# A Fourier filter and a gated MLP on one core: the opening's pieces in another order, the identity matrix made by POOL instead of loaded

## The chip, the cores and the metric

The kernel runs on one core of a Trainium2 chip. The metric is the device time of one execution in microseconds; the median of three runs is compared. A profiled execution has its own device time and, inside it, a span from its first to its last instruction. Engines: PE multiplies matrices (PEld loads its weights), DVE works elementwise, ACT evaluates functions, POOL does small copies and sums over partitions, SP issues the DMAs. Each engine works through its own queue in order; they wait for one another through semaphores.

## The reference

```python
xn = layernorm(x)                                # x is [1, 2048, 448], f32
A  = irfft2(rfft2(xn) * (w_r + 1j * w_i))        # over the 2048 rows and 448 columns
g  = xn @ W_gate;  u = xn @ W_up                 # [448, 1792] each
B  = (where(g > 0, g, 0) * u) @ W_down           # [1792, 448]
return x + A + B
```

## The kernel before

Every f32 operand of a matmul is split into a high and a low f16 part, and each product is three f16 passes. The 2048 rows lie as 16 row tiles of 128 partitions, numbered n2; tiles n2, n2+4, n2+8, n2+12 form a chunk q, and the chunks are worked in the order 0, 2, 1, 3. A row tile is normalised, split (`hi`, `lo`), and transposed into `Tq[q]`, [128, 9, 512]. The 1792 hidden columns are 14 tiles f in groups of 5, 5 and 4; a *unit* is one f with one chunk q: 20 matmuls of 128x512 and its share of four half passes into the PSUM tile `gu` (g=0 gate, g=1 up). A weight tile `wst` (256 KB) is squared and summed by ACT (`w_sq`), summed over partitions by POOL (`w_sum`, a PartitionAllReduce), turned into a power of two by DVE (`w_scale`), and split by ACT (`w_hi`) and DVE (`w_lo`) into the f16 tile `wt`. The second matmul with `W_down` (`dn`) and the Fourier part (`fx`) follow chunk by chunk, woven into the units by a planner that spends estimated costs (`add(cost, ...)`, `run_bg`).

The first five units cannot be planned that way, because rows and weights arrive while they are used. So a string, `OPENING`, names small pieces one after the other, and inside `tc.manual_schedule` each engine gets its instructions in exactly that order. `lx4` loads row tile 4, `lw` the next weight tile, `st4` its statistics, `sqA`/`rsA` the reciprocal deviation of tiles 0 and 4 (`B`: 8 and 12), `xn4` the normalised f32 row, `hi4`/`lo4` the split, `cp4` two POOL copies inside the split tile, `tpA4`/`tpB4` transposes on PE against an identity matrix `id_t`, `vevA4`/`aevA4` the evictions to `Tq` by DVE or ACT, `wsqW0g1`, `parW0g1`, `wscW0g1`, `whiW0g1`, `wloW0g1` the five weight steps, `hh10`, `lh10`, `hl10` parts of unit 0 (first digit g, second the half of the 512 columns), `gu1g0` half g=0 of unit 1, `kwN` and `warm` matmuls on a zero tile that nothing reads.

Of the kernel before, what the change touches and what calls it, by code (L numbers as in the profile page):

```python
# [8 lines left out]

# [16 lines left out]
NWARM = 19  # L26
# [4 lines left out]
lx0 lx4 lw lid lw lx8 lx12 lw lw lw lw lx2 lx10 lx6 lx14 lwd0 lwd1 lwd2 lwd3 lwd4 warm st0 st4 sqA rsA hi4  # L31
xn4 xn0 wsqW0g0 cp4 st8 hi0 parW0g0 st12 wsqW0g1 cp0 tpA0 lo0 tpA4 kw1 wscW0g0 sqB tpB0 kw6 parW0g1 wsqW1g0
rsB whiW0g0 vevB0 lo4 wsqW1g1 xn12 tpB4 kw3 hi8 parW1 wscW0g1 xn8 whiW0g1 cp8 vevA0 vevA4 hi12 tpA8 vevB4
hh10 hh00 lo8 wsqW2g1 cp12 tpA12 hl00 lo12 aevA12 tpB8 aevA8 hl10 wloW0g0 lw aevB8 tpB12 wscW1 lh00 aevB12
wloW0g1 lw lfd hh01 hh11 whiW1g0 st2 lh01 lh10 whiW1g1 hl01 wloW1g0 lw hl11 wsqW2g0 wloW1g1 lw ly0 ly4 ly8
ly12 d90 d94 d98 d912 lh11 wsqW3g0 st10 parW2 hp0 st14 wsqW3g1 gu1g0 st6 wdq0 parW3 wscW2 sqC wscW3 whiW2g0 rsC gu1g1 re0
wloW2g0 whiW3g1 tm0 whiW2g1 xn6 wsqW4g0 xn2 gu2g0 wloW2g1 hi2 re1 xn10 gh0 wloW3g1 whiW3g0 tm1 gu2g1 wdq1
wloW3g0 hi10 xn14 lo2 hi14 hi6 cp14 hp2 wsqW4g1 cp2 lo6 gu3g0 cp10 dm2 lo14 re2 parW4 wdq2 cp6 wscW4 tm2
whiW4g0 dm14 lo10 wdq4 gu3g1 wloW4g0 gh1 dm10 gl0 whiW4g1 gl1 dm6 gu4g0 re3 wloW4g1 wdq3 tm3 wdp gh3
wdsc gh2 gu4g1 gl2 wdh1 wdh2 wdl1 wdh0 wdl2 hp4 gl3 re4 wdh3 tm4 wdl0 gh4 wdh4 gl4 wdl3 wdl4  # L40
# [43 lines left out]
def _constants():  # L84
# [55 lines left out]
    ident = np.eye(128, dtype=np.float16)  # L140
    return dict(ident=ident, c_fd=c_fd, c_fm=np.ascontiguousarray(c_fm), c_im=c_im, c_row=c_row,
# [4 lines left out]
def tile_gfnet_reglu(ctx: ExitStack, tc: tile.TileContext, x, xr, wgu, wd, wf, ident, c_fd, c_fm, c_im, c_row, c_id,  # L146
# [100 lines left out]
    def ln_stats(q, j):  # L247
        n2 = q + 4 * j
        st = ft([128, 6], F32, "bst", 2)
        V.bn_stats(st, xr_t[n2])  # L250
        if j == 0:
            mv[q] = ft([128, 4, 2], F32, "mv", 2)
        V.bn_aggr(mv[q][:, j, :], st)

    rst = {}

    def ln_sd(q, js=(0, 1, 2, 3)):
        w = ft([128, 5, 4], F32, "rs", 3)
        n = len(js)
        rst[q, js[0]] = w[:, :, 0:n], mv[q][:, js[0]:js[-1] + 1, :]  # L260
        A.activation(w[:, 0, 0:n], rst[q, js[0]][1][:, :, 1], AF.Sqrt, bias=eps)

    def ln_rstd(q, js=(0, 1, 2, 3), bias=False):
        w, m = rst[q, js[0]]
        sd, r0, t, r, nm = (w[:, i] for i in range(5))
        V.reciprocal(r0, sd)
        V.scalar_tensor_tensor(t, m[:, :, 1], 1e-5, r0, op0=OP.add, op1=OP.mult)
        V.scalar_tensor_tensor(t, t, -0.5 * 2048, r0, op0=OP.mult, op1=OP.mult)
        V.scalar_tensor_tensor(r, t, 1.5 * 2048, r0, op0=OP.add, op1=OP.mult)
        if bias:  # L270
            V.scalar_tensor_tensor(nm, m[:, :, 0], -1.0, r, op0=OP.mult, op1=OP.mult)
        elif q in CHUNKS[2:]:
            V.tensor_scalar(nm, m[:, :, 0], -1.0, None, op0=OP.mult)
        for i, j in enumerate(js):
            rst[q, j] = r[:, i:i + 1], nm[:, i:i + 1], m[:, i, 0:1]
# [9 lines left out]

    def ln_xn(n2):
        xn_b[n2] = free.pop(0)
        xn[n2] = xn_b[n2].rearrange("p g c k -> p (g c k)")[:, 0:D]
        r, _, mean = rst[n2 % 4, n2 // 4]
        V.tensor_scalar(xn[n2], xr_t[n2], mean, r, op0=OP.subtract, op1=OP.mult)  # L290

    def ln_hi(n2, fused=False):
        new_tt(n2)
        o = tt[n2].rearrange("p a b -> p (a b)")[:, 0:D]
        r, nm, _ = rst[n2 % 4, n2 // 4]
        if fused:
            A.activation(o, xr_t[n2], AF.Identity, scale=r, bias=nm)
        else:
            A.activation(o, xn[n2], AF.Copy)
# [6 lines left out]
    def ln_norm(n2):  # L306
        xn_b[n2] = free.pop(0)
        xn[n2] = xn_b[n2].rearrange("p g c k -> p (g c k)")[:, 0:D]
        r, nm, _ = rst[n2 % 4, n2 // 4]
        A.activation(xn[n2], xr_t[n2], AF.Identity, bias=nm)  # L310
        new_tt(n2)
        A.activation(tt[n2].rearrange("p a b -> p (a b)")[:, 0:D], xn[n2], AF.Copy, scale=r)
        ln_copy(n2)
        free.append(xr_b.pop(n2))

    def ln_lo(n2):
        x, t = xn[n2], tt[n2].rearrange("p a b -> p (a b)")
        x2, t2 = [v[:, None, :].to_broadcast([128, 2, 64]) for v in (x[:, 384:448], t[:, 384:448])]
        if n2 % 4 in CHUNKS[2:]:
            r = rst[n2 % 4, n2 // 4][0]  # L320
            V.scalar_tensor_tensor(t[:, 512:896], x[:, 0:384], r, t[:, 0:384], op0=OP.mult, op1=OP.subtract)
            V.scalar_tensor_tensor(tt[n2][:, 3:9:5, 64:128], x2, r, t2, op0=OP.mult, op1=OP.subtract)
        else:
            V.tensor_tensor(t[:, 512:896], x[:, 0:384], t[:, 0:384], op=OP.subtract)
            V.tensor_tensor(tt[n2][:, 3:9:5, 64:128], x2, t2, op=OP.subtract)
        G.tensor_copy(tt[n2][:, 8, 0:48].rearrange("p (a b) -> p a b", b=16), tt[n2][:, 4:7, 112:128])
        free.append(xn_b.pop(n2))

# [351 lines left out]
    def w_scale(f, gs=(0, 1)):  # L680
        sc = mt([128, 2], F32, "wsc", 6)
        e = eg[:, f, gs[0]:gs[-1] + 1]
        half_exponent(e, state["wm", f][:, 1, gs[0]:gs[-1] + 1])
        shift_exponent(sc[:, 0:len(gs)], e, -1, 188)
        for i, k in enumerate(gs):
            wsc[f, k] = sc[:, i:i + 1]

# [8 lines left out]
    def wd_sq(i, f):  # L696
        if i == 0:
            state["wdm"] = mt([128, 2, NR], F32, "wdm", 1)
        squares(wdst[f], state["wdm"][:, 0, i:i + 1])
# [43 lines left out]
    def gu_half(f, q, g, start, prev):  # L743


        rows, b = TOP[g]
        m = P.matmul(hps[f, q][:, g, 0:512], wt[f, g][rows, 7, :], Tq[q][rows, b, :], start=start, stop=not start).ins  # L747
# [17 lines left out]
    def gu_halves(f, q, mate):  # L765
        gu_open(*mate)
        m = last["P"]
        for i in range(4):
            with tc.high_priority(offset=2000 if i else 0):
                m = gu_half(*((f, q) if i > 1 else mate), 1 - i % 2, i < 2, m)  # L770
        opened.add(mate)
# [81 lines left out]
    def ln_chunk(q):  # L853
        for j in range(4):
            add(0.63, ln_stats, q, j)
        add(0.0, ln_sd, q)
        add(0.6, ln_rstd, q)
# [194 lines left out]
    def keep_warm(n):  # L1052
        for _ in range(n):
            P.matmul(wps, warm[:, 0:128], warm, start=True, stop=True)

    pieces = {"lid": lambda: nc.sync.dma_start(id_t, ident), "lfd": lambda: nc.sync.dma_start(fd_t, c_fd),
              "lw": load_wn, "warm": lambda: keep_warm(NWARM),
              **{f"kw{n}": (lambda n=n: keep_warm(n)) for n in (1, 3, 6)},
# [3 lines left out]
    def piece(name, fn, *a):  # L1062
        pieces[name] = lambda: fn(*a)

    for c, q in enumerate(CHUNKS[:2]):
        for js, tag in (((0, 1), "A"), ((2, 3), "B")) if c == 0 else (((0, 1, 2, 3), "C"),):
            piece("sq" + tag, ln_sd, q, js)
            piece("rs" + tag, ln_rstd, q, js, c == 0)
        for j in range(4):
            n2 = q + 4 * j  # L1070
            for tag, fn, *a in (("lx", load_xr), ("ly", load_x), ("st", ln_stats, j), ("xn", ln_xn),
                                ("hi", ln_hi, c == 0), ("cp", ln_copy), ("lo", ln_lo), ("dm", ln_dma), ("d9", ln_dma9),
                                ("tpA", ln_tp, (0, 1, 2)), ("tpB", ln_tp, (4, 5, 6, 3, 7))):
                piece(f"{tag}{n2}", fn, *((q,) if tag == "st" else (n2,)), *a)
# [5 lines left out]
    def gu_slab(f, g):  # L1080
        if f % 2 == 0 and g == 0:
            gu_open(f, q)
        gu_full(f, q, (g,), slice(0, 512), f % 2 == 0, f % 2 == 1)

    for f in groups[0]:
# [5 lines left out]
        piece(f"wscW{f}", w_scale, f)  # L1091
# [4 lines left out]
        for g in range(2):  # L1096
# [4 lines left out]
            if f == 0:  # L1101
                piece(f"parW{f}g{g}", w_sum, f, (g,))
                piece(f"wscW{f}g{g}", w_scale, f, (g,))
# [4 lines left out]
    with tc.manual_schedule(engines={mybir.EngineType.PE, mybir.EngineType.DVE, mybir.EngineType.Activation,  # L1108
# [4 lines left out]
        gu_open(0, q)  # L1113
        for name in OPENING.split():
            pieces[name]()
# [64 lines left out]
_ORDER = ["x", "xr", "wgu", "wd", "wf", "ident", "c_fd", "c_fm", "c_im", "c_row", "c_id"]  # L1180
# [42 lines left out]
```

## Time and profile before

| what | value |
|---|---|
| median of 3 runs | 447.95 us (447.57 to 448.4) |
| profiled execution, device time | 448.09 us |
| its span | 446.3 us |
| PE busy in the span | 437.7 us (98%) |
| DVE, ACT, POOL busy | 381.9, 188.2, 34.3 us |
| first matmul into `gu` | 14.44 us after the span's start |

The 1.8 us between device time and span lie around the first and last instruction. "Idle before, releaser" names the instruction whose end let a waiting engine go on. Durations of single instructions overlap a little with the next one on the same engine.

### The profile page before, as it was taken

The page shows a single profiled execution, that of the slowest core. Times are in us where ns is not written, and L with a number is a line of the kernel's source. Part 1 is how long each engine was busy: PE and PEld are TensorE (multiplying, and loading weights), DVE is VectorE, ACT ScalarE, POOL GpSimd, SP SyncE. Part 2 cuts the span into 40 slices and gives each one's busy share as a digit, 9 for nine tenths or more (in the row PEclk, how much of TensorE's full clock was granted, in tenths as well). Part 3 has the DMA queues.
Part 4 walks back from the last instruction along what each step waited for, and adds up shares of the span by engine and source line. Part 5 has one row for each costly group of instructions (what it writes and reads, how often), then busy time and mean ns, then how long its engine had stood idle before and what let it go on. Part 6 is the DMA issues. An engine that isn't in the chain of part 4 may idle for free.

```text
span 446.3 us, 7350 instructions
## 1 busy us (share of the span) xinstructions
PE 437.7 (98%) x2625; PEld 219.1 (49%) x2625; DVE 381.9 (86%) x958; ACT 188.2 (42%) x398; POOL 34.3 (8%) x89
## 2 busy tenths in 40 slices
PE   6999999999999999999999999999999999999996
PEld 2544555545455444444444444444445555555654
DVE  5989698999858899999999999987998799875443
ACT  5887263732643774323132255263334133244130
POOL 2320030210000310000000310100000000000000
PEclk9999999999999999999999999999999999999999
DMA  7939985040001462431302100011121121101212
GB/s 248 312 88 269 368 266 116 16 92 2 1 2 48 140 198 81 133 117 45 98 29 85 41 0 2 0 43 63 41 71 35 58 79 35 53 13 50 82 47 82
DMA packets 39228, 39.61 MB, mean 89 GB/s; under 512 B 18470, under 2 KB 35096, under 8 KB 39192
## 3 DMA queue, kind: packets, MB, share of 16 engines
q1 hardware_dynamic: 39192, 39.15, 28.6%
q8 instruction: 20, 0.33, 0.3%
q14 instruction: 16, 0.13, 0.1%
HBM read 24.38 MB, written 3.67 MB: 63 GB/s over the span
## 4 chain that ended last, share of the span: by engine, by line
PE 91%; DMA 3%; DVE 3%; issue 1%; SPq 0%; ACT 0%; POOL 0%; DVEq 0%; ACTq 0%
PE gu L740 51%; PE dn L808 26%; PE gu L747 3%; PE fx L639 2%; PE fx L368 2%; PE fx L658 2%; DMA wst<-in_wgu 2%; PE fx L398 2%; DMA y<-in_xr 1%; PE dn L836 1%; DVE wt L694 1%; PE gu L836 1%; DVE g L781 0%; DVE y L290 0%; DVE xy L814 0%
## 5 line engine op out<-in xcount | busy, mean ns | idle before, releaser
L740 PE MATMUL gu<-T,wt 128*128 128x512 f16 (+1 forms) x1140 | 255.6, 375 | 0.2 <-DVE wt L694 0.2
L740 PEld LDWEIGHTS <-wt 128*128 128x128 f16 x1140 | 108.7, 98 | 130.7 <-issue 9.8
L808 PE MATMUL dn<-wdt,h 128*128 128x448 f16 x624 | 127.0, 352 | 0.0
L808 PEld LDWEIGHTS <-h 128*128 128x128 f16 x624 | 60.3, 98 | 56.4 <-issue 0.4
L777 ACT ACTIVATE g<-gu 128x512 f32<-128x512 f32 x56 | 33.2, 593 | 92.4 <-PE gu L747 54.3
L785 ACT ACTIVATE h<-g 128x512 f16<-128x512 f32 x56 | 34.9, 626 | 58.2 <-DVE g L781 58.1
L781 DVE SCALAR_TENSOR_TENSOR g<-gu,g 128x512 f32<-128x512 f32 x56 | 38.3, 684 | 15.3 <-ACT g L777 15.2
L789 DVE TENSOR_TENSOR h<-g,h 128x512 f16<-128x512 f32 x56 | 38.3, 685 | 8.2 <-ACT h L785 8.0
L814 DVE SCALAR_TENSOR_TENSOR xy<-dn,dsc,xy 128x448 f32<-128x448 f32 x46 | 31.0, 676 | 12.3 <-PE dn L808 7.8
L189 POOL PARTITION_ALL_REDUCE wm<-wm x15 | 11.7, 779 | 167.8 <-ACT junk L186 167.8
L623 ACT ACTIVATE vt<-y,fsc 128x456 f16<-128x456 f32 x16 | 10.8, 673 | 27.9 <-PE fx L639 23.7
L690 ACT ACTIVATE wt<-wst,wsc 128x512 f16<-128x512 f32 x28 | 19.3, 714 | 5.6 <-DVE wsc L196 5.6
L694 DVE SCALAR_TENSOR_TENSOR wt<-wst,wsc,wt 128x512 f16<-128x512 f32 x28 | 20.4, 744 | 0.0
L186 ACT ACTIVATE junk<-wst 128x512 bf16<-128x512 f32 x28 | 17.4, 621 | 0.2
L747 PE MATMUL gu<-T,wt 64*128 64x512 f16 x112 | 17.0, 381 | 0.1
L663 DVE SCALAR_TENSOR_TENSOR xy<-fx,fsc,xy 128x448 f32<-128x448 f32 x16 | 10.8, 680 | 7.2 <-PE fx L658 7.2
L389 ACT ACTIVATE Xh<-X 128x456 f16<-128x456 f32 x16 | 9.3, 579 | 17.7 <-DVE X L387 8.7
L404 DVE TENSOR_TENSOR y<-y,y 128x456 f32<-128x456 f32 x22 | 13.8, 627 | 0.2
L639 PEld LDWEIGHTS <-vt 128*128 128x128 f16 x192 | 12.0, 98 | 4.0 <-issue 0.8
L250 DVE BATCH_NORM_STATS2 bst<-y 128x6 f32<-128x448 f32 x16 | 9.7, 612 | 4.9 <-DMA y<-in_xr 4.9
L405 DVE TENSOR_TENSOR y<-y,y 128x456 f32<-128x456 f32 x22 | 13.8, 626 | 0.1
L639 PE MATMUL fx<-im,vt 128*128 128x128 f16 x192 | 13.5, 219 | 0.0
(131 smaller groups left out, 476.9 us busy)
## 6 DMA issues: line engine op xcount, KB each, us to landing
sw<-y SPq DMA_DIRECT2D x64, 112.2 KB
wst<-in_wgu SPq DMA_DIRECT2D x28, 256.0 KB
wf<-in_wf SPq DMA_DIRECT2D x16, 228.0 KB
y<-in_xr SPq DMA_DIRECT2D x16, 224.0 KB
xy<-in_x SPq DMA_DIRECT2D x16, 224.0 KB
out<-xy SPq DMA_DIRECT2D x15, 224.0 KB
wdst<-in_wd SPq DMA_DIRECT2D x14, 224.0 KB
fm<-in_c_fm SPq DMA_DIRECT2D x4, 256.0 KB
```

The source lines that it names most:

```text
L186: A.activation(mt([128, 512], BF16, "junk")[:, 0:src.shape[-1]], src, AF.Square, scale=SQ, accum_out=acc)
L639: P.matmul(o, v[:, h, w], m[:, c, :], start=(i == 0), stop=(i == 2), skip_group_check=True)
L690: A.activation(w[:, 0:4, :], wst[f, g], AF.Copy, scale=wsc[f, g])
L694: V.scalar_tensor_tensor(w[:, 4:8, :], st, sc, w[:, 0:4, :], op0=OP.mult, op1=OP.subtract)
L740: last["P"] = P.matmul(hps[f, q][:, g, cs], wt[f, g][:, a, :], Tq[q][:, b, cs], start=(start and i == 0), stop=(stop and i == len(seq) - 1 ...
L747: m = P.matmul(hps[f, q][:, g, 0:512], wt[f, g][rows, 7, :], Tq[q][rows, b, :], start=start, stop=not start).ins
L777: last["A"] = A.activation(g1s[f, q], hps[f, q][:, 0, :], AF.Relu, scale=2.0 ** -22).ins
L781: last["V"] = V.scalar_tensor_tensor(g1, hps[f, q][:, 1, :], 2.0 ** -22, g1, op0=OP.mult, op1=OP.mult).ins
L785: A.activation(ht[f, q][:, 0, :], g1s[f, q], AF.Copy)
L789: V.tensor_tensor(h[:, 1, :], g1s.pop((f, q)), h[:, 0, :], op=OP.subtract)
L808: last["P"] = P.matmul(ps[:, 0:D], ht[f, q][:, a, js], wdt[f][:, b, :], start=(i == 0), stop=(i == n - 1)).ins
L814: last["V"] = V.scalar_tensor_tensor(xy[:, n2, cs], dps[n2][:, cs], dsc[:, g:g + 1], xy[:, n2, cs], op0=OP.mult, op1=OP.add).ins
```

## The change

The string is replaced. In words:

- The four row tiles of chunk 0 are loaded ahead of the first weight tiles; the other rows, the `xy` tiles, `fd_t` and the `W_down` tiles come later among the weights.
- `id_t` is no longer loaded (`lid`): the piece `mkid` has POOL clear it and write the diagonal with an affine select.
- Statistics, deviation and weight scale become pieces of one instruction each (`bn`/`ag`, `ra` to `rd`, `wex`/`wsc`), `lo` becomes `lo`/`lp`; the negated mean is its own piece `ng`.
- Row tiles 0 and 4 are centred by ACT (`xc`) and scaled by the split; tiles 8 and 12 and chunk 2 are normalised by DVE (`xn`) and copied by ACT.
- Unit 1 is issued in six pieces (`uh`, `um`, `ul` for each g) instead of two, some of them ahead of unit 0's half passes.
- 24 matmuls on the zero tile at the start and 4 later, instead of 19 and 10.
- Later chunks take their statistics two tiles at a time.

```diff
-NWARM = 19
+NWARM = 24
-lx0 lx4 lw lid lw lx8 lx12 lw lw lw lw lx2 lx10 lx6 lx14 lwd0 lwd1 lwd2 lwd3 lwd4 warm st0 st4 sqA rsA hi4
-xn4 xn0 wsqW0g0 cp4 st8 hi0 parW0g0 st12 wsqW0g1 cp0 tpA0 lo0 tpA4 kw1 wscW0g0 sqB tpB0 kw6 parW0g1 wsqW1g0
...
+lx0 lx4 bn0 bn4 ag0 ag4 warm ngA lx8 lx12 sqA xc0 xc4 raA rbA rcA rdA bn8 hi0 cp0 lw lw mkid lw bn12 hi4 ag8 cp4 lw
+tpA0 ag12 lo0 tpA4 sqB lp0 raB wsqW0g1 parW0g1 lx2 tpB0 lo4 lp4 lw wsqW0g0 rbB vevB0 wexW0g1 rcB parW0g0 wsqW1g0
+tpB4 kw4 vevA0 rdB wscW0g1 lw wexW0g0 whiW0g1 lw vevA4 wscW0g0 xn12 hh10 whiW0g0 vevB4 hl10 lx14 xn8 hh00 lw hl00
...
+    def ln_xc(n2):
+        xn_b[n2] = free.pop(0)
+        xn[n2] = xn_b[n2].rearrange("p g c k -> p (g c k)")[:, 0:D]
+        A.activation(xn[n2], xr_t[n2], AF.Identity, bias=rst[n2 % 4, n2 // 4, "m"])
...
+        A.activation(tt[n2].rearrange("p a b -> p (a b)")[:, 0:D], xn[n2], AF.Copy, scale=rst[n2 % 4, n2 // 4])
...
-    pieces = {"lid": lambda: nc.sync.dma_start(id_t, ident), "lfd": lambda: nc.sync.dma_start(fd_t, c_fd),
+    pieces = {"mkid": lambda: make_identity(nc, id_t), "lfd": lambda: nc.sync.dma_start(fd_t, c_fd),
...
+    def gu_part(g, n):
+        if (1, q) not in hps:
+            gu_open(1, q)
+        gu_full(1, q, (g,), slice(0, 512), n == 0, n == 2, (seq1[0:3], seq2, seq1[3:6])[n])
```

The function that `mkid` calls, on a [128, 128] f16 tile (sq is 128):

```python
def make_identity(nc, identity):
    nc.gpsimd.memset(identity, 0.0)
    nc.gpsimd.affine_select(out=identity, in_=identity, compare_op=mybir.AluOpType.not_equal, fill=1.0,
                            base=0, pattern=[[-1, sq]], channel_multiplier=1)
```

What the edit becomes on POOL is seen only in the program that is built from it. POOL before, from the first row copy to the second partition sum (`tt` are the split row tiles, `wm` the sums of squares; the plain `ISA` row is an instruction that names the code library that POOL needs next, here the one with index 1):

```order
L303 COPY tt0_100<-tt0_100 128x48 [waits Activation_49]
L304 COPY tt0_100<-tt0_100 128x64
L189 ISA
L189 ISA wm_182<-wm_182 128x1 [waits Activation_49]
L303 COPY tt1_101<-tt1_101 128x48 [waits Activation_49]
L304 COPY tt1_101<-tt1_101 128x64
L326 COPY tt1_101<-tt1_101 128x48 [waits DVE_49]
L189 ISA wm_182<-wm_182 128x1 [waits Activation_49]
```

It stands once, ahead of the first of 15 partition sums. POOL after, the same place (the library named ahead of the select has index 0, the one ahead of the sum index 1):

```order
L329 COPY tt0_100<-tt0_100 128x48 [waits Activation_49]
L330 COPY tt0_100<-tt0_100 128x64
masks.py:197 MEMSET id_t_97 128x128
masks.py:199 ISA
masks.py:199 AFFINE_SELECT id_t_97<-id_t_97 128x128 [waits Pool_49]
L329 COPY tt1_101<-tt1_101 128x48 [waits Activation_49]
L330 COPY tt1_101<-tt1_101 128x64
L354 COPY tt0_100<-tt0_100 128x48 [waits DVE_49]
L190 ISA
L190 ISA wm_199<-wm_199 128x1 [waits Activation_49]
L354 COPY tt1_101<-tt1_101 128x48 [waits DVE_49]
L190 ISA wm_199<-wm_199 128x1 [waits Activation_49]
```

The identity and a second library row now stand between the first row copy and the first partition sum. DVE before, around the first weight scale (`eg`, `wsc` from the sums `wm`; `rs` the deviations, `mv` the statistics; `T0` is the transposed chunk, `fx` the transposes' PSUM):

```order
L325 TENSOR_TENSOR tt1_101<-y9_75,tt1_101 128x2x64
L192 TENSOR_SCALAR eg_89<-wm_182 128x1 [waits Pool_49]
L196 TENSOR_SCALAR wsc_211<-eg_89 128x1 [waits DVE_49]
L266 RECIPROCAL rs_214<-rs_214 128x2 [waits Activation_49]
L267 SCALAR_TENSOR_TENSOR rs_214<-mv_167,rs_214 128x2 [waits DVE_49]
L268 SCALAR_TENSOR_TENSOR rs_214<-rs_214 128x2 [waits DVE_49]
L269 SCALAR_TENSOR_TENSOR rs_214<-rs_214 128x2 [waits DVE_49]
L271 SCALAR_TENSOR_TENSOR rs_214<-mv_167,rs_214 128x2 [waits DVE_49]
L352 COPY T0_62<-fx_199 128x5x128 [waits PE_49]
```

Both steps of the scale stood together, ahead of the first eviction. DVE after, the same place:

```order
L384 COPY T0_62<-fx_184 128x5x128 [waits PE_49]
L193 TENSOR_SCALAR eg_89<-wm_199 128x1 [waits Pool_49]
L287 SCALAR_TENSOR_TENSOR rs_194<-rs_194 128x2 [waits DVE_49]
L384 COPY T0_62<-fx_184 128x3x128
L291 SCALAR_TENSOR_TENSOR rs_194<-rs_194 128x2 [waits DVE_49]
L197 TENSOR_SCALAR wsc_235<-eg_89 128x1
L193 TENSOR_SCALAR eg_89<-wm_199 128x1 [waits Pool_49]
L384 COPY T0_62<-fx_190 128x3x128 [waits PE_49]
```

The two steps of the scale (L193, L197) stand apart now, with an eviction between them, and the first eviction has moved ahead of the read of the first partition sum. DVE's other evictions for unit 0, both low weight parts and the two `xn` rows are queued behind that read.

More of the change, by code (lines that the diff above doesn't have):

```diff
@@ L8 @@
 from concourse._compat import with_exitstack
+from concourse.masks import make_identity
 F16 = mybir.dt.float16
@@ L257, in ln_sd @@
+    bst, rst, whole = {}, {}, set()
     def ln_sd(q, js=(0, 1, 2, 3)):
-        w = ft([128, 5, 4], F32, "rs", 3)
         n = len(js)
-        rst[q, js[0]] = w[:, :, 0:n], mv[q][:, js[0]:js[-1] + 1, :]
-        A.activation(w[:, 0, 0:n], rst[q, js[0]][1][:, :, 1], AF.Sqrt, bias=eps)
-    def ln_rstd(q, js=(0, 1, 2, 3), bias=False):
-        w, m = rst[q, js[0]]
[L265 to L273, printed above, removed]
+        w = ft([128, 5, 4], F32, "rs", 3)[:, :, 0:n]
+        rst[q, js[0]] = w, mv[q][:, js[0]:js[-1] + 1, :]
+        A.activation(w[:, 0], mv[q][:, js[0]:js[-1] + 1, 1], AF.Sqrt, bias=eps)
```

160 lines of the change are left out of this document (98 added, 62 removed).

## Prediction, written before the changed kernel ran

> **What bounds the kernel now.** I read the windows first, with edges where the trace changes character: the first matmul of unit 0, the end of the first five units, the tail. Columns are the stretch, its length, busy time with instruction count per engine, granted clock, DMA share, GB/s.
>
> ```profile
> core 0: us, PE busy (x) PEld busy (x) DVE busy (x) ACT busy (x) POOL busy (x), PEclk, DMA share, GB/s
> 0.00:14.44 14.44, 9.91 (x48) 4.09 (x49) 9.02 (x35) 8.28 (x18) 4.08 (x20) 1.00 0.85 282
> 14.44:45.00 30.56, 30.28 (x175) 15.04 (x173) 28.48 (x73) 25.66 (x56) 6.16 (x20) 1.00 0.72 206
> 45.00:400.00 355.00, 355.00 (x2072) 174.84 (x2071) 322.18 (x817) 143.28 (x308) 24.06 (x49) 1.00 0.25 74
> 400.00:446.30 46.30, 42.52 (x339) 25.09 (x336) 22.18 (x35) 10.97 (x18) 0.00 (x0) 0.99 0.18 64
> ```
>
> From 14.44 to 400 us PE idles 0.28 us in all. The edit leaves the useful matmuls as they are: unit 0 in its parts, unit 1 as 2 x 10, the half passes, everything later. So the time after is the time before plus the shift of PE's first useful matmul plus any new gap behind it. The second look is PE's timeline over that first stretch (start, length, what, idle before it with releaser).
>
> ```profile
> 1.54 6.10 PE L1054 MATMUL dn<-warm 128*128 128x512 f16 x19 [1.54 <-POOL warm L1111]
> 8.37 0.51 PE L344 MATMUL fx<-id_t,tt 128*128 128x128 f16 x6 [0.73 <-ACT tt L297]
> 10.43 0.49 PE L344 MATMUL fx<-id_t,tt 128*128 128x128 f16 x5 [1.34 <-DVE tt L324]
> 14.44 0.81 PE L740 MATMUL gu<-T,wt 128*128 128x256 f16 x6
> 20.51 8.81 PE L740 MATMUL gu<-T,wt 128*128 128x512 f16 x40
> ```
>
> All before 14.44 is filling and transposes. What must happen first is a chain over five engines: rows land, statistics, split, transpose; and a weight tile lands, is squared, summed over partitions by POOL, scaled by DVE, split by ACT. POOL's timeline is the third look, since the identity and the partition sums meet there.
>
> ```profile
> 0.96 0.53 POOL L1111 MEMSET warm<- 128x512 f16 x1
> 7.12 0.23 POOL L303 COPY tt<-tt 128x48 f16<-128x48 f16 x1 [5.63 <-ACT tt L297]
> 7.27 0.24 POOL L304 COPY tt<-tt 128x64 f16<-128x64 f16 x1
> 7.76 0.40 POOL L189 PARTITION_ALL_REDUCE wm<-wm  x1 [0.25 <-ACT junk L186]
> 8.38 0.22 POOL L303 COPY tt<-tt 128x48 f16<-128x48 f16 x1 [0.22 <-ACT tt L297]
> ```
>
> The program before has one row that names a code library, between the copy at 7.27 and the sum at 7.76. The copy ends at 7.51, so the row can have cost 0.25 us at most, and ACT's square is named as what ended that gap. But the only library this program ever names is the one its own last execution left behind. This row prices naming a library that lies there; it does not price a change.
>
> **The change, part by part.** Up to POOL's first copy nothing gets slower. Tiles 0 and 4 are still first in SP's queue, and the same four statistics end at 4.94 (the last aggregate below); the deviation starts at 4.98 in both.
>
> ```profile
> 4.76 0.18 DVE L253 BATCH_NORM_AGGREGATE mv<-bst 128x2 f32<-128x6 f32 x1
> 4.98 0.30 ACT L261 ACTIVATE rs<-mv,eps 128x2 f32<-128x2 f32 x1 [2.75 <-DVE mv L253]
> 57.22 2.33 ACT L310 ACTIVATE y<-y,rs 128x448 f32<-128x448 f32 x4
> 6.29 0.76 ACT L297 ACTIVATE tt<-y,rs 128x448 f16<-128x448 f32 x1 [1.02 <-DVE rs L271]
> 6.96 0.61 ACT L186 ACTIVATE junk<-wst 128x512 bf16<-128x512 f32 x1
> ```
>
> Centring on ACT costs 0.58 a tile by the third row (later chunks do it so): 5.28 + 2 x 0.58 = 6.44, and the split of tile 0, taken at 0.58 too, ends at 7.02, as in the fourth row. DVE's four reciprocal steps run beside it. POOL's first copy is at 7.1 again. Removing the 32 KB identity load frees one issue slot of SP and about 0.1 us of transfer; loading tiles 8 and 12 ahead of the weights delays the first weight. Before, the fifth transfer (992 KB summed) landed at 7.05 and the sixth (1216 KB) let DVE go on at 8.36:
>
> ```profile
> 2.60 4.45 DMA wst<-in_wgu
> 8.36 0.63 DVE L250 BATCH_NORM_STATS2 bst<-y 128x6 f32<-128x448 f32 x1 [1.26 <-DMA y<-in_xr]
> 7.07 5.71 DMA y<-in_xr
> 12.80 4.87 DMA wst<-in_wgu
> ```
>
> W0g1, which is now squared first, completes 1408 KB, another 192 KB at the window's 282 GB/s, so it lands near 9.0. Three squares at 0.7 then keep ACT until 11.1. With POOL free, its sum would run 9.8 to 10.2, DVE's scale with the eviction and deviation steps between takes 0.75, ready 11.0, ACT's split (0.65) ends 11.75, and unit 0 starts at 11.85: 2.6 us early. That is the whole good side of the change.
>
> Now POOL's new rows. Behind the copies (7.51): a clear of 128x128, 0.1; the change to library 0, price t; the select, 0.3 (between the 0.24 of a 64-wide copy and the 0.53 of a 512-wide clear); two copies for tile 4, 0.4; one for the low part, 0.2; the change back to library 1, t; the sum, 0.4. Sum over at 8.9 + 2t. Every engine queues behind this. PE's transposes wait for the identity; DVE's next row reads the sum, with six of unit 0's eight evictions and both low weight parts behind it; ACT's next row is the split, which waits for the scale. From there, as above, 0.1 + 0.75 + 0.7 + 0.15: unit 0 starts at 10.6 + 2t, or at 11.85 if that is later. It equals the 14.44 of before at t = 1.9.
>
> What is t? The trace does not show a change. From below: 0, since the one library row cost under 0.25. In between: ACT's table load, an engine's tables fetched before its first function, 1.28 us. [...]
>
> ```profile
> 0.74 1.28 ACT L1110 ACT_TABLE_LOAD   x1 [0.74 <-PEq L1211]
> 10.00:15.00 5.00, 3.65 (x28) 1.99 (x29) 4.79 (x20) 4.38 (x10) 1.93 (x6) 1.00 1.05 396
> ```
>
> [...] Both changes are needed in every execution, because each ends with library 1. Unit 0 then starts at 22.0, 7.6 us late.
>
> [...]
>
> Behind the start two smaller losses. PE is empty from about 8.9 (24 filler matmuls) until the transposes and four fillers near 14, then again until 22. Its first matmuls are slow:
>
> ```profile
> 4.50 0.15 PEld L1054 LDWEIGHTS <-warm 128*128 128x128 f16 x1 [0.28 <-issue]
> 4.93 0.15 PEld L1054 LDWEIGHTS <-warm 128*128 128x128 f16 x1 [0.28 <-issue]
> ```
>
> Loads stand 0.43 us apart until 4.93, against 8.81/40 = 0.22 later, though the granted clock reads 1.00 throughout. Nine such are 1.9 us lost. No gap in this trace is long enough to show whether it comes back after idling, so 0 to 1.9; of the full amount about half hides, as unit 0's later parts wait for DVE's low weights anyway: 0.9. [...] The second loss is a wait of 0.4 for the low tiles of the second row: DVE evicts them after both scales and one `xn` row. The rest of the ramp has the same DVE and ACT work per unit as before (28.48 of 30.56 and 25.66 of 30.56 busy), shifted as a whole; splitting unit 1 in six and the pairs of statistics later are costed at nothing, hidden by PE's work, 355.00 of 355.00 us.
>
> Sum: 7.6 + 0.9 + 0.4 = 8.9 us. The profiled execution took 448.09 (span 446.3), 0.14 above the median of 447.95, so 457.0 by its own time and 456.9 by the median.
>
> **Rivals.** First, the faster side: a change of library is free, as the 0.25 us gap reads if taken literally. Then POOL is never late and unit 0 starts 2.6 early: 447.95 - 2.6 = 445.4. It decides wherever t stays under 1.9; a table-load price of 1.28 would still gain, 10.6 + 2.6 = 13.2, so 446.7. For it: the only row that exists. Against it: that row does not show a change.
>
> Second, one change instead of two, if library 0 is in place at the start of each execution. Unit 0 then starts at 10.6 + 5.71 = 16.3, 1.9 late, and with half the small losses 450.5. Against it: then the sum of before at 7.76 would already have paid one.
>
> [...]
>
> Fourth, that the earlier start is real and DVE gives it back: it is 93% busy from 14.44 to 45, so feeding PE 2.6 us sooner needs work that is not done. Then about 448, no change.
>
> **How the numbers follow.** Forecast, two changes near 5.7 each (451 to 459.4, for t from 2.8 to 7.0): 0.62. Free or nearly so: 0.16. One change: 0.06. Dearer: 0.13. Given back: 0.03. The range reaches from the free case to the dear end of the third rival, 445.2 to 462, and leaves out about half of the free case's spread and what is dearer still; the likeliest case's own is 451 to 459.4. A change under 0.2% (0.9 us) is about what a measurement of this kernel can't tell from none. Faster by more: the free case and its neighbours, 0.16. Within: given back and a sliver of t near 1.9, 0.04. Slower: the rest, 0.80.
>
> **What would show it.** In the trace after, POOL should be without a row for 5 to 6 us between the clear of `id_t` and the select, and again between the low-part copy and the first partition sum; PE's transposes should wait for POOL until about 13.5 and DVE's first scale until about 20. The first matmul into `gu` should stand near 22, with weight loads 0.4 us apart around it. The windows beyond should have PE full as before. If the select follows the clear within a microsecond, the forecast is wrong by its largest term. If POOL is prompt and unit 0 still starts late, the weights' landing or DVE's queue is the cause, and if the gaps are there but the end is not late, PE had slack that I read as work.

## The result, and the profile after

The changed kernel takes 462.76 us (median of 4 runs, 462.34 to 464.89) against 447.90 us (447.57 to 448.40) for the kernel before: 1.0347 times as long, 95% interval 1.0313 to 1.0380. The forecast was 456.9 us with a range up to 462. The direction and the largest term, two changes of library, came as forecast; the time is 5.9 us longer than forecast and 0.8 us past the range. The profiled execution took 464.89 us, 2.1 above its median, with a span of 463.1 us against 446.3: it has 16.8 us to explain. A second trace of the same kernel, below, tells which part of that belongs to the one execution.

POOL's timeline after, first the two places where the forecast put a change of code library (start, length, what, idle before it with releaser):

```profile
7.21 0.21 POOL masks.py:197 MEMSET id_t<- 128x128 f16 x1
15.74 0.28 POOL masks.py:199 TENSOR_SCALAR_AFFINE_SELECT id_t<-id_t 128x128 f16<-128x128 f16 x1 [8.32 <-issue]
...
16.34 0.21 POOL L354 COPY tt<-tt 128x48 f16<-128x48 f16 x1
22.35 0.40 POOL L190 PARTITION_ALL_REDUCE wm<-wm  x1 [5.81 <-issue]
```

Both gaps are there, and "issue" says that POOL waited for no other engine. They are 8.32 and 5.81 us, not 5.71 each. Behind the sum stand DVE's scale and ACT's split, as the prediction said, each with its wait (DVE, then ACT):

```profile
22.79 0.15 DVE L193 TENSOR_SCALAR eg<-wm 128x1 uint32<-128x1 uint32 x1 [4.85 <-POOL wm L190]
```

```profile
23.44 1.33 ACT L727 ACTIVATE wt<-wst,wsc 128x512 f16<-128x512 f32 x2 [12.66 <-DVE wsc L197]
```

PE's timeline after. The rows marked L784 are the half passes, of which the opening has three sets of four; they are the landmarks that both kernels share (before: 19.97, 29.25 and 38.87).

```profile
16.07 1.86 PE L376 MATMUL fx<-id_t,tt 128*128 128x128 f16 x16 [6.97 <-POOL id_t masks.py:199]
...
24.22 3.17 PE L777 MATMUL gu<-T,wt 128*128 128x256 f16 x14 [4.57 <-ACT wt L727]
...
41.63 0.61 PE L784 MATMUL gu<-T,wt 64*128 64x512 f16 x4
42.17 8.81 PE L777 MATMUL gu<-T,wt 128*128 128x512 f16 x40
53.12 0.61 PE L784 MATMUL gu<-T,wt 64*128 64x512 f16 x4 [2.14 <-DMA T<-tt]
53.66 6.18 PE L777 MATMUL gu<-T,wt 128*128 128x512 f16 x20
```

Three things are to be seen. Unit 0 starts at 24.22 instead of 14.44. Its 14 matmuls of 128x256 take 3.17 us, 0.226 each, where six took 0.81 before. And the third half passes wait 2.14 us for a DMA transpose, after which 20 matmuls take 6.18 us; in before the same 20 took 4.49:

```profile
29.25 0.61 PE L747 MATMUL gu<-T,wt 64*128 64x512 f16 x4
...
38.87 0.61 PE L747 MATMUL gu<-T,wt 64*128 64x512 f16 x4
39.41 4.49 PE L740 MATMUL gu<-T,wt 128*128 128x512 f16 x20
```

The windows put a granted clock to both slow stretches of after (stretch, length, PE busy and count, clock, DMA share, GB/s):

```profile
24.20:30.00 5.80, 5.78 (x31) 0.50 0.54 174
30.00:45.00 15.00, 15.00 (x89) 1.00 0.54 160
45.00:60.00 15.00, 12.86 (x54) 0.89 0.88 235
```

So the whole difference can be read as a shift against before at five places: unit 0's first matmul (before 14.44), the second half passes (29.25), the third (38.87), the end of the 20 matmuls behind them (39.41 + 4.49 = 43.90), and the span (446.3). The experiments below are set in the same table, each with its one profiled execution (those of e3 and e6 lie some 2.5 and 1.2 us below their medians); differences between neighbouring columns say where time went.

| kernel | unit 0 starts | 2nd half passes | 3rd half passes | 20 behind end | span |
|---|---|---|---|---|---|
| after | +9.78 | +12.38 | +14.25 | +15.94 | +16.8 |
| after, second trace (e13) | +10.78 | +12.51 | +14.46 | +14.46 | +15.9 |
| e5, more filler matmuls | +10.78 | +11.62 | +12.15 | +12.15 | +14.1 |
| e14, e5 with both repairs | +11.15 | +12.09 | +12.72 | +12.72 | +13.9 |
| e2, before with POOL's identity | +12.34 | +12.33 | +12.35 | +12.35 | +12.4 |
| e3, identity first in the string | +4.22 | +6.47 | +6.73 | +6.73 | +8.5 |
| e1, identity loaded | -3.14 | -2.31 | +0.33 | +1.92 | +3.1 |
| e4, no library change | -2.68 | -1.86 | +0.08 | +0.07 | +2.4 |
| e6, e4 with `W_down` loads ahead | -3.06 | -2.15 | -1.66 | -1.66 | +0.1 |
| e7, e4 with old statistics | -2.16 | -1.34 | +0.62 | +0.62 | +1.6 |
| e8, e4 with both repairs | -2.70 | -1.79 | -1.31 | -1.31 | -0.4 |
| e10, e8 with identity loaded | -2.43 | -1.34 | -0.78 | -0.78 | +0.5 |
| e11, e10 with later statistics | -2.41 | -1.49 | -0.96 | -0.96 | -0.9 |

Read by its first row: 9.78 before the start, 2.60 up to the second half passes, 1.87 up to the third, 1.69 in the matmuls behind, 0.86 in all that follows.

### The profile page after: what moved, and what is told of

The parts are those of the page before. It is cut to its first block, busy times and chain, and to the rows that moved or that the text cites. A ratio compares the mean times of both kernels' runs of the same rounds, so it can differ in the third digit from the quotient of the medians.

```text
span 463.1 us, 7351 instructions
## 1 busy us (share of the span) xinstructions
PE 443.8 (96%) x2624; PEld 222.0 (48%) x2624; DVE 380.4 (82%) x958; ACT 187.5 (40%) x397; POOL 39.7 (9%) x91
## 4 chain that ended last, share of the span: by engine, by line
PE 82%; DVE 7%; issue 5%; DMA 2%; SPq 2%; POOL 1%; ACT 0%; DVEq 0%; POOLq 0%; ACTq 0%
PE gu L777 45%; PE dn L847 24%; PE gu L784 3%; PE fx L671 2%; PE fx L690 2%; PE fx L430 2%; PE fx L400 2%; PE dn L875 1%; DMA T<-tt 1%; SPq L370 1%; DVE g L820 1%; DVE xy L853 1%; DVE tt L341 1%; DMA wdst<-in_wd 1%; DMA y<-in_xr 1%
## 5 line engine op out<-in xcount | busy, mean ns | idle before, releaser
L777 PE MATMUL gu<-T,wt 128*128 128x512 f16 (+1 forms) x1140 | 259.5, 380 | 4.7 <-ACT wt L727 4.6
L777 PEld LDWEIGHTS <-wt 128*128 128x128 f16 x1140 | 110.6, 99 | 137.9 <-issue 12.7
L190 POOL PARTITION_ALL_REDUCE wm<-wm x15 | 15.1, 1004 | 175.0 <-ACT junk L187 169.2
L784 PE MATMUL gu<-T,wt 64*128 64x512 f16 x112 | 17.0, 381 | 2.1 <-DMA T<-tt 2.1
L671 PE MATMUL fx<-im,vt 128*128 128x128 f16 x192 | 13.5, 219 | 0.0
```

The costliest lines, as they stand in the source:

```text
L671: P.matmul(o, v[:, h, w], m[:, c, :], start=(i == 0), stop=(i == 2), skip_group_check=True)
L777: last["P"] = P.matmul(hps[f, q][:, g, cs], wt[f, g][:, a, :], Tq[q][:, b, cs], start=(start and i == 0), stop=(stop and i == len(seq) - 1 ...
```

## The experiments

### What making the identity costs, and why

e2 is the kernel before with one edit, the identity made by POOL:

```diff
-lx0 lx4 lw lid lw lx8 lx12
+lx0 lx4 lw lw lx8 lx12
...
-xn4 xn0 wsqW0g0 cp4 st8 hi0 parW0g0
+xn4 xn0 wsqW0g0 cp4 mkid st8 hi0 parW0g0
...
-    pieces = {"lid": lambda: nc.sync.dma_start(id_t, ident),
+    pieces = {"mkid": lambda: make_identity(nc, id_t),
```

> The kernel before with one edit: the identity is not loaded but made by POOL behind its first copies; the old order otherwise. Theory L: two gaps on POOL of 6 to 8 us, the first partition sum at 21 to 23 instead of 7.8, unit 0 near 26 to 28 instead of 14.4, time 459 to 463 us: the whole loss from this edit alone. Rival O (the order loses, library changes are hidden): 447.5 to 449.

Measured: 460.93 us (460.53 to 461.96), ratio 1.0298 [1.0284, 1.0311], in theory L's range. POOL of it, then PE:

```profile
15.24 0.28 POOL masks.py:199 TENSOR_SCALAR_AFFINE_SELECT id_t<-id_t 128x128 f16<-128x128 f16 x1 [7.57 <-issue]
21.48 0.40 POOL L190 PARTITION_ALL_REDUCE wm<-wm  x1 [5.96 <-issue]
```

```profile
26.78 0.82 PE L741 MATMUL gu<-T,wt 128*128 128x256 f16 x6
51.22 0.61 PE L748 MATMUL gu<-T,wt 64*128 64x512 f16 x4
```

This one piece alone costs 13.0 us, where the whole change costs 14.9. In the table its row is flat: 12.34 at the start, 12.35 at the third half passes, 12.4 at the end. The order of before carries a late start to the end without adding to it, and its first six matmuls of unit 0 take 0.82 us, so PE is not slow there. Whatever grows along a row of the other kernels comes with the new order, its fewer filler matmuls behind the transposes included.

e3 is the kernel after with `mkid` as the first piece of the string, so that the first change runs while the rows land.

```diff
-lx0 lx4 bn0 bn4 ... cp0 lw lw mkid lw bn12
+mkid lx0 lx4 bn0 bn4 ... cp0 lw lw lw bn12
```

> The changed kernel with POOL's identity first in the string, no sum ahead of it: both library changes stay, the first starts at 1.5 us instead of 7.4. Theory L: select near 9 to 10, first copies behind it, second change from about 11 to 17 to 19, unit 0 near 19 to 21, 457 to 460 us. Rival S (the select is slow, wherever it is): only the gap before the select moves, second gap stays; 455 to 460. If both changes depend on what the DMAs carry, the first gap here is shorter than 8.3, since few transfers are under way.

Measured: 459.15 us (456.6 to 460.5), ratio 1.0264 [1.0245, 1.0284]. POOL, then PE:

```profile
9.67 0.33 POOL masks.py:199 TENSOR_SCALAR_AFFINE_SELECT id_t<-id_t 128x128 f16<-128x128 f16 x1 [8.05 <-issue]
...
16.80 0.40 POOL L190 PARTITION_ALL_REDUCE wm<-wm  x1 [5.89 <-issue]
```

```profile
18.66 3.17 PE L777 MATMUL gu<-T,wt 128*128 128x256 f16 x14 [6.69 <-ACT wt L727]
...
45.60 0.61 PE L784 MATMUL gu<-T,wt 64*128 64x512 f16 x4 [0.53 <-DMA T<-tt]
```

Both changes are still paid; 3.6 us come back because part of the first lies in time in which nothing could have been done anyway. The string has no earlier place for it. The time fits theory L and rival S alike; the next run separates them.

e4 puts a partition sum of a constant ahead of `mkid`, again first in the string. It adds one small instruction and leaves nothing out.

```diff
-    "mkid": lambda: make_identity(nc, id_t)
+    "mkid": lambda: (all_sum(mt([128, 1], F32, "sum0"), eps), make_identity(nc, id_t))
```

> The changed kernel with POOL's identity first in the string and one partition sum of a constant ahead of it; the library with index 1, which the sums use, carries the select too, so the program names that library once and never changes. Theory L: POOL has the identity by 2.6 us, no gap, time 445.4 us as with the loaded identity. Rival S (the select, not the change of library, takes the 8.3 us): POOL's first copy at 10 or later, 451 to 455. Rival O: 450 to 458 as with the loaded identity.

Measured: 450.73 us (450.04 to 451.27), ratio 1.0067 [1.0055, 1.0079]. POOL, then PE:

```profile
1.62 0.40 POOL L190 PARTITION_ALL_REDUCE sum<-eps  x1
1.88 0.27 POOL masks.py:197 MEMSET id_t<- 128x128 f16 x1
2.23 0.29 POOL masks.py:199 TENSOR_SCALAR_AFFINE_SELECT id_t<-id_t 128x128 f16<-128x128 f16 x1
```

```profile
11.76 1.81 PE L777 MATMUL gu<-T,wt 128*128 128x256 f16 x14 [0.73 <-DVE y L317]
...
38.95 0.61 PE L784 MATMUL gu<-T,wt 64*128 64x512 f16 x4 [1.54 <-DMA T<-tt]
```

With the sum first, the same select follows without any gap (the clear ends at 2.15, the select starts at 2.23): it runs from the library of the sum, and no change is needed. So the price is one of changing libraries and not of the select. With no price left, unit 0 starts at 11.76 (the prediction's good side said 11.85), and yet the kernel is 0.67% slower than before: the 445.4 of theory L did not come, and the time lies in rival O's range. By the third half passes the 2.68 us of lead are gone, and another 2.3 go after that.

e1 removes POOL's work instead, by loading the identity behind the first two row tiles, as a DMA like that of before.

```diff
-lx0 lx4 bn0 bn4 ... lw lw mkid lw
+lx0 lx4 lid bn0 bn4 ... lw lw lw
```

> The changed kernel with the identity loaded by a DMA behind the first two row tiles and no POOL identity, so no change of library. Theory L (the two library changes, 8.3 and 5.8 us in the changed kernel's trace, are the loss): first partition sum near 9.9, unit 0 near 11.9, time 445.4 us, 2.6 under the kernel before. Rival O (the new order itself loses, by rows ahead of weights or DVE's queue): slower than 447.9, 450 to 458. Rival D (the earlier start is given back by DVE): 447.4 to 448.4.

Measured: 450.94 us (448.4 to 452.32), ratio 1.0065 [1.0042, 1.0089], as e4: two ways to be rid of the changes, one time. In its profiled execution the third half passes wait longer, and PE is slow behind them:

```profile
39.20 1.04 PE L785 MATMUL gu<-T,wt 64*128 64x512 f16 x4 [2.79 <-DMA T<-tt]
40.16 5.66 PE L778 MATMUL gu<-T,wt 128*128 128x512 f16 x20
```

The granted clock from 39.2 to 45.0 us is 0.71 there, and 1.00 in e4, where the wait was 1.54.

e9 asks what a change costs elsewhere: before, with one small addition on POOL behind the sum of the eighth weight tile, near 118 us.

```diff
         all_sum(m[:, 1, g], m[:, 0, g])
+        if f == 7:
+            G.tensor_tensor(mt([128, 2], F32, "twice"), m[:, 1, g], m[:, 1, g], op=OP.add)
```

> The kernel before with one edit: near 118 us, behind the partition sum of weight tile 7, POOL adds that sum to itself into a tile that nobody reads, an operation of library 0, so the program changes to library 0 there and back to 1 for the next sum, where DMAs are busy for 0.07 of the time. It prices both changes away from the opening's transfers and under cover. Theory K (the price hangs on which library is called, not on the stream): 7.5 to 8.3 us ahead of the addition, 5.8 to 6.0 ahead of the next sum, time 447.7 to 448.3. Rival M (the stream makes the first change dear): both 5.8 to 6.0. Rival (a change stops other engines too): 455 or more.

Measured: 447.73 us (447.07 to 448.12), ratio 0.9998 [0.9989, 1.0007]. The gaps are 7.55 us before the addition and 5.90 before the next sum, as theory K had them, and the time doesn't change: POOL has nothing due there. e12 repeats it for every weight tile from the eighth on (`if f >= 7`), to get several prices in one execution.

> The kernel before with a small tensor_tensor on POOL behind the partition sum of every weight tile from the eighth on, so that POOL goes to the other library and back some six times between 118 and 300 us; nothing reads its result. Theory A (each library has a price of its own): the gaps ahead of the tensor_tensor lie at 7.5 to 8.3 and those ahead of the sums at 5.8 to 6.0, wherever the DMA share is high or low. Theory B (the price follows the DMA stream at that moment, or simply varies): gaps of both kinds spread over 5.5 to 9 without order. Where two tiles follow each other within 14 us PE may now wait, so the time is 448 to 465 and says nothing.

Measured: 471.64 us in one execution, slower than the range given. Only the gaps are used. POOL of it:

```profile
125.23 0.18 POOL L680 TENSOR_TENSOR twice<-wm 128x2 f32<-128x2 f32 x1 [7.37 <-issue]
138.96 0.18 POOL L680 TENSOR_TENSOR twice<-wm 128x2 f32<-128x2 f32 x1 [7.17 <-issue]
266.33 0.19 POOL L680 TENSOR_TENSOR twice<-wm 128x2 f32<-128x2 f32 x1 [6.88 <-issue]
287.19 0.41 POOL L189 PARTITION_ALL_REDUCE wm<-wm  x1 [6.11 <-issue]
300.85 0.41 POOL L189 PARTITION_ALL_REDUCE wm<-wm  x1 [5.94 <-issue]
308.18 0.18 POOL L680 TENSOR_TENSOR twice<-wm 128x2 f32<-128x2 f32 x1 [6.93 <-issue]
314.26 0.40 POOL L189 PARTITION_ALL_REDUCE small<-small  x1 [5.89 <-issue]
```

Where POOL waited for nothing else, the six gaps towards the addition are 6.70 to 7.37 at a DMA share of 0.00 to 0.01 (theory A's bounds were too high). Those back to the sum are 5.89, 5.94 and 6.11, and one of 6.40 with a share of 0.50 from 157.0 to 166.1 us. The two libraries differ, as theory A says. For the sum's library the opening is no dearer (5.81 to 5.97 in after, e2, e3, e5, e13 and e14). For the other it is: 7.57, 8.05, 8.32, 9.12, 9.31 and 9.63 in e2, e3, after, e5, e13 and e14, up to 2.9 us above the lowest price of e12. That the DMA stream adds this is not shown: e2 paid 7.57 at a DMA share of 1.02 and e9 7.55 at 0.01, and the dearest three stand at 0.62 to 0.69. What sets it stays open.

### Where the lead of e4 goes

Before issues its five `W_down` loads in a row; the new string issues the first behind `d90` and `d98` and the other four behind all of the small DMA transposes `d90` to `d912`. SP before, then SP after, then ACT after and in e4:

```profile
9.62 2.90 SPq L236 DMA_DIRECT2D wdst<-in_wd  x5
...
30.79 6.02 SPq L334 DMA_TRANSPOSE T<-tt  x4
```

```profile
37.88 0.91 SPq L237 DMA_DIRECT2D wdst<-in_wd  x2
45.07 5.84 SPq L366 DMA_TRANSPOSE T<-tt  x4
```

```profile
43.08 0.58 ACT L187 ACTIVATE junk<-wdst 128x448 bf16<-128x448 f32 x1 [0.70 <-DMA wdst<-in_wd]
```

```profile
29.66 0.58 ACT L187 ACTIVATE junk<-wdst 128x448 bf16<-128x448 f32 x1 [1.19 <-DMA wdst<-in_wd]
```

ACT's squares of `W_down` wait for their loads, the splits of chunk 2 stand in ACT's queue among them, and the transposes that PE's third half passes read follow. In before the transposes go out 16.35 us after unit 0's start (30.79), in e4 19.4 (31.16). e6 is e4 with the five loads right behind `d90`:

```diff
-wloW0g1 wloW0g0 d90 lh10 ... hl11 lwd4 wsqW3g0 ... whiW3g0 lwd1 lwd2 ul0 ... lo6 lwd3 lp6 ... wdq3 lwd0 gu2g0
+wloW0g1 wloW0g0 d90 lwd4 lwd1 lwd2 lwd3 lwd0 lh10 ... hl11 wsqW3g0 ... whiW3g0 ul0 ... lo6 lp6 ... wdq3 gu2g0
```

> The kernel without a library change (partition sum ahead of the select, 450.73 us) with one more edit: the five W_down loads stand right behind the first small transpose on SP, instead of behind the other three. Theory Q (the second loss: the W_down tiles wait in SP's queue behind small transposes, their squares hold ACT's queue, chunk 2's split and its big transposes are late, PE waits 1.5 us for them near 37): ACT's 1.2 us wait for W_down goes, chunk 2's transposes start 1.0 to 1.5 us earlier, 449.0 to 449.8 us. Rival T (DVE's queue sets chunk 2, since it is busy from 24 to 33 without a gap over 0.4): the loads land earlier and nothing moves, 450.5 to 451.

Measured: 449.36 us (448.2 to 449.81), ratio 1.0036 [1.0023, 1.0049], 1.4 below e4, as theory Q had it. The wait falls from 1.54 to 0.40:

```profile
37.21 0.61 PE L784 MATMUL gu<-T,wt 64*128 64x512 f16 x4 [0.40 <-DMA T<-tt]
```

The second place is near 73 us. Later chunks take their statistics two tiles at a time; DVE reaches one whose rows have not landed, and the sums that PE's transforms read are queued behind it. DVE, then PE's waits, in e4:

```profile
72.83 0.63 DVE L250 BATCH_NORM_STATS2 bst<-y 128x6 f32<-128x448 f32 x1 [5.25 <-DMA y<-in_xr]
...
74.57 0.62 DVE L474 TENSOR_TENSOR y<-y,fx 128x456 f32<-128x456 f32 x1
```

```profile
PE fx L400 <- DVE y L474: 1.7, 1, 1.7
```

e7 is e4 with the later chunks planned as in before:

```diff
-        for js in ((0, 1), (2, 3)):
-            add(1.24, ln_stats, q, js)
+        for j in range(4):
+            add(0.63, ln_stats, q, (j,))
         add(0.0, ln_sd, q)
-        add(0.1, ln_neg, q)
         add(0.6, ln_rstd, q)
+        add(0.0, ln_neg, q)
```

> The kernel without a library change (450.73 us) with one more edit: later chunks take their statistics one row tile at a time under the old planner costs, as before the change. Theory P (a third loss: PE waits 1.7 us at 73 for DVE, because the later statistics are planned differently): that wait goes, 448.8 to 449.2 us. Rival H (the wait at 73 is handed down from a late opening): it stays, 450.4 to 451.

Measured: 449.15 us (447.7 to 449.7), ratio 1.0027 [1.0016, 1.0038], 1.6 below e4, as theory P had it; this wait falls to 0.6 and the one at the half passes stays, at 1.56. The two repairs touch different places, so e8 has both.

> Both edits, the W_down loads ahead and the old costs for later statistics. Theories Q and P together: 447.2 to 448.2 us, level with the kernel before. Rivals T and H together: 450.3 to 451.

Measured: 447.55 us (447.08 to 448.55, 11 runs) against 447.86, ratio 0.9997 [0.9988, 1.0005]. They add up (1.4 and 1.6, together 3.2), and the kernel is level with before although unit 0 starts 2.7 us earlier. Two waits remain, 0.4 at the half passes and 0.5 near 72 us, where DVE still stands before an unlanded row:

```profile
71.32 0.63 DVE L250 BATCH_NORM_STATS2 bst<-y 128x6 f32<-128x448 f32 x1 [2.58 <-DMA y<-in_xr]
```

e10 is e8 with the identity loaded as in e1, and e11 is e10 with those statistics pushed later:

```diff
-            add(0.63, ln_stats, q, (j,))
+            add(1.3 if q == 1 else 0.63, ln_stats, q, (j,))
```

> The kernel after with the identity loaded by DMA behind the first two row tiles (no work of POOL for it), the five W_down loads right behind the first transpose issue on SP, and the later chunks' statistics one tile at a time with their costs of before. Unit 0 should start near 11.3 instead of 11.74. Theory (the start of unit 0 no longer sets the end; DVE and the transposes of chunk 2 do): as the kernel with the last two of these edits and a warm-library select, 447.5. Rival (every tenth of an earlier start counts): 447.1 or less.

> The kernel with the identity loaded, the W_down loads ahead and the old costs, and the four statistics of chunk 1 given a cost of 1.3 instead of 0.63 in the planner, so that they stand later among the other work. Before this edit DVE waits 2.6 us near 69 us for a row tile that has not landed, with the sums that PE's transforms read queued behind it. Theory (that wait is the last of the loss behind the opening, some 0.5 to 0.7 us): PE's wait near 72 goes and the time is 446.8 to 447.0. Rival (the order of planned work has slack, or other work moves into the way): 447.5, as without the edit.

Measured: e10 448.33 us (447.14 to 451.43), ratio 1.0013 [0.9999, 1.0028]. Unit 0 started at 12.01, not at 11.3, so this run says nothing on what an earlier start is worth; loading the identity is no better than the select behind a sum. e11: 447.17 us (446.89 to 447.91, 11 runs) against 447.85, ratio 0.9988 [0.9980, 0.9997]. The time lies between the theory's 447.0 and the rival's 447.5. The wait near 72 is gone, and these are all that PE has from 24 to 110 us:

```profile
PE gu L785 <- DMA T<-tt: 0.4, 1, 0.4
PE gu L778 <- DVE g L821: 0.2, 1, 0.2
```

e11 is the fastest kernel of the study, 0.12% below before, with an interval that only just leaves out no change. So that is what the rest of the new order is worth, freed of POOL's identity and three side effects: of a lead of 2.41 us at the start, 0.9 us reach the end of the span.

### What PE's idling costs, and the sum

e5 is the kernel after with more matmuls on the zero tile, to keep PE busy through both gaps.

```diff
-NWARM = 24
+NWARM = 55
-tpB4 kw4 vevA0
+tpB4 kw24 vevA0
```

> The kernel after with more filler matmuls, nothing else: 55 in place of 24 at the start and 24 in place of 4 behind the first transposes, so that PE does not stand empty before unit 0. Unit 0 should start where it did, near 24.2, since POOL's two gaps (8.32 and 5.81) are untouched. Theory (an idle PE comes back slow, and that is part of what was lost behind the start): the first matmuls of unit 0 are spaced 0.11 instead of 0.22 us, about 2.1 of the 2.8 us lost between 24.2 and 30 come back, and the time is about 460.7. Rival (unit 0's parts wait for the low weights and DVE anyway, so that the slow PE is hidden): 462.4 to 462.8, as after.

Measured: 462.52 us (462.12 to 463.37), ratio 1.0330 [1.0317, 1.0343]. This is the rival's time, and beside the 462.76 of after it would say that the slow PE costs nothing. The trace says that it does, and that this execution paid for it elsewhere: its first library change took 9.12 us, and unit 0 started at 25.22.

```profile
25.22 1.83 PE L777 MATMUL gu<-T,wt 128*128 128x256 f16 x14 [2.07 <-ACT wt L727]
```

```profile
25.22:30.00 4.78, 4.58 (x46) 1.00 0.45 135
```

The clock is 1.00 where it was 0.50, and the 14 matmuls take 1.83 us instead of 3.17. A fair comparison needs the kernel after with the same start. e13, the kernel after once more with no edit, happened to give one. Beside it ran e14, which is e5 with the two repairs of e8:

```diff
-NWARM = 24
+NWARM = 55
-tpB4 kw4 vevA0
+tpB4 kw24 vevA0
-wloW0g1 wloW0g0 d90 lh10
+wloW0g1 wloW0g0 d90 lwd4 lwd1 lwd2 lwd3 lwd0 lh10
...
-            add(1.24, ln_stats, q, js)
+            add(0.63, ln_stats, q, (j,))
```

> The kernel after, unchanged, for a second trace of it. The profiled execution of the first took 464.9 against a median of 462.8. If the 2.1 us between them is PE gone cold again at chunk 2's half passes, a trace near the median shows a wait below 3 us there and matmuls at 0.22 behind it. If it is the price of the library changes, the gaps of POOL add up to about 12 instead of 14.1. Time: 462.3 to 465.

> The kernel after with everything mended but the two library changes: more filler matmuls (55 and 24), the W_down loads ahead on SP, the statistics of later chunks one tile at a time at their old costs. Theory (with the losses behind the start gone, the end shifts one for one with the start of unit 0): against 447.5 with unit 0 at 11.74, a start at 24.2 to 25.2 gives 460.0 to 461.0. Rival (the losses behind the start were only slack that the late start had made, and the price of the changes sets the end): 462.5, as with more filler alone.

Measured on one chip, which is not that of e5: e13 464.14 us (463.82 to 464.45), ratio 1.0370 [1.0353, 1.0388], so the same kernel took 1.4 us longer than when it was first measured; e14 461.98 us (460.29 to 462.28), ratio 1.0313 [1.0293, 1.0334]. POOL, then PE of e13:

```profile
16.72 0.28 POOL masks.py:199 TENSOR_SCALAR_AFFINE_SELECT id_t<-id_t 128x128 f16<-128x128 f16 x1 [9.31 <-issue]
```

```profile
25.22 3.17 PE L777 MATMUL gu<-T,wt 128*128 128x256 f16 x14 [4.59 <-ACT wt L727]
53.33 0.61 PE L784 MATMUL gu<-T,wt 64*128 64x512 f16 x4 [2.03 <-DMA T<-tt]
53.87 4.49 PE L777 MATMUL gu<-T,wt 128*128 128x512 f16 x20
```

With both at 25.22, e5 reaches the second half passes 0.9 us earlier than e13, the third 2.3 earlier, and ends 1.8 earlier (spans 460.4 and 462.2). Its transposes also go out earlier, at 43.19 against 45.54. So in this pair a PE gone slow costs 0.9 us directly, and about as much again is lost behind it. That the second part follows from the first is not shown beyond the pair: in e3 the 14 matmuls took 3.17 us too, and the third half passes waited only 0.53. The two library gaps of after add up to 14.13 us in its first trace and to 15.13 in e13 (15.09 in e5), which moves the start of unit 0 by 1 us between executions of one kernel. e13's 20 matmuls took 4.49 us, so the 1.69 us of a second slow stretch behind the third half passes belong to the first trace and not to every execution of the kernel.

e14 starts unit 0 at 25.59, 13.85 us later than e8. One for one that makes 447.75 + 13.85 = 461.6 for the profiled execution; it took 462.03, and the median is 461.98. The rival's 462.5 is as near to the median, so the time alone doesn't decide. The table says more: e14 and e5 end 0.2 us of span apart with starts 0.37 apart, so the two repairs that brought 3.2 us in e8 bring some 0.6 here. The rival was right in this: most of what they mend is covered when the start is late and PE is kept busy. Of what the edits bring back in the kernel after, the slow PE is the larger part. But e14 still ends 13.9 late where it starts 11.15 late: 2.75 us behind the start are brought back by none of them. PE's wait for the transposes is 0.55 of it; the rest was not followed.

## Why the prediction was wrong

**The price of a change** (forecast 5.71 twice, measured 8.32 and 5.81). Two changes, in the order named, no row for them, everything behind them: that came. The size did not. The 5.71 us is the time of one DMA of before, that of a row tile (7.07 to 12.78), and was the author's estimate for each change; no run shows it as the price of a change, and the runs showed 5.81 to 6.40 us towards the sum's library and 6.70 to 9.63 towards the other. The two changes have prices of their own. That the sum's library came within 0.3 us of that row in the openings is luck, since it costs as much where the DMA engines are idle (5.94 and 6.11 at a share of 0.00 in e12); the other is 1 to 4 us dearer. That moved unit 0's start from the forecast 22.0 to 24.22, 2.2 us of the 7.9 by which the profiled execution exceeds the forecast by its own time; of the rest, 1.3 fall to the next paragraph and 4.4 to the one behind it. (With the measured gaps, 10.6 + 2t gives 24.7: the rest of that chain was 0.5 us too long.) That the changes are dearer had a chance of 0.13, and it is the case that came: the two gaps add up to 14.13 and 15.13 us in the two traces. The dear end of the range, 462, still fell short, for the next two reasons.

**The slow PE and the low tiles** (forecast 0.9 + 0.4, measured 1.7 to 2.6 between the start and the second half passes). That PE comes back slow after idling was weighed between 0 and 1.9 and taken at half; the pair e5 and e13 shows 0.9 directly, as forecast, while in the first trace, where the clock stays at 0.50 to 30 us, the column is 0.9 longer still. The rest of this column, 0.8 to 1.1, is in every kernel with the new order, early start or late, and stands where the prediction had 0.4. The pair also shows transposes issued 2.3 us later and a wait of 2.0 instead of 0.5, which e3, with PE as slow, doesn't have. As for the idling: in after, unit 0's first matmuls ran at a clock of 0.50 (24.20 to 30.00 us) behind waits of 6.97 and 4.57 us. At the third half passes PE was slow behind the wait in two executions (2.14 us in after, 2.79 in e1) and not in two others (1.54 in e4, 2.03 in e13).

**"Shifted as a whole", costed at nothing** (measured 3.4 us in the second trace, 4.4 in the first). This is the step that failed in its reasoning and not in a size. The argument was that DVE and ACT have the same work per unit as before. It looked at how much each engine does and not at what its queue waits for. SP's queue was not walked: the `W_down` loads moved behind the small transposes and so made ACT, and through it the transposes of chunk 2, late. Nor was it asked whether rows have landed when DVE meets the pair statistics of chunk 1. e6 and e7 show both, 1.4 and 1.6 us, with an early start; behind the late start of the kernel after they count for less. Of the 3.4 us of the second trace, 2.5 remain in e5, without the slow PE, and 1.8 in e14, with the two repairs as well. So over half of this loss is something that no run took away behind a late start (the edit of e11 was not tried there), and its cause stays open.

**The good side.** Unit 0 at 11.85 with POOL free came out as 11.76. But the sentence that a start 2.6 us early is 2.6 us gained was wrong: e4 and e1, with the price of the changes at nothing, are 0.67 and 0.65% slower than before. The first rival's 445.4 would have missed by over 5 us even with its premise true. The fourth rival, that the lead is given back, named the outcome; its reason, DVE's load, was at most part of it, since two repairs on SP and in the planner brought 3.2 us back.

**What would show it.** POOL's two gaps, the transposes held by POOL (16.07, forecast 13.5), DVE's first scale (22.79, forecast 20) and slow matmuls around unit 0's start all came. That the windows beyond have PE full as before did not: from 45 to 60 us it is busy 12.86 of 15.00.

## What to carry to other kernels

An instruction that moves POOL from one code library to another cost 5.8 to 9.6 us here, in both directions and with no row of its own; look in the trace for which library is in place, and let the helper run from that one (one partition sum ahead of the select took the 8.4 us from e3 to e4) or let the change fall where POOL has nothing due (e9, with 7.55 and 5.90 us of gaps, ran at 0.9998 of the time of before). When an order is rewritten, walk each queue with the landing times of what it waits for, the DMA queue first: equal busy time says nothing about who stands behind whom. And compare two orders by their shift at a few shared landmarks: an early start is worth only what is left of it at the last one.

## What the runs showed of the hardware

- The price of a change differs by library: 5.81 to 6.40 us towards the partition sum's, wherever it was measured; 6.70 to 7.55 towards the other with the DMA engines idle (share 0.00 to 0.01 in e9 and e12), 7.57 to 9.63 in the opening.
- The affine select, which waited 7.57 us and more where no sum had gone ahead of it (e2, e3, after, e5, e13, e14), ran without a gap (clear at 1.88, select at 2.23) behind a partition sum in e4.
- PE's granted clock was below 1.00 (0.50 from 54 to 57 us in after, 0.71 as the mean from 39.2 to 45.0 in e1) after waits of 2.14 and 2.79 us in the middle of work and stayed at 1.00 after 1.54 (e4, 39.2 to 45.0) and 2.03 (e13, 53.8 to 58.4); 2.14 and 2.03 are the same wait in two executions of the kernel after. Whether the length of the wait alone decides was not tested.
